# A new replayed order, with smaller edits at the start, in a two-layer kernel of windowed attention and token mixing

## The chip, the cores and the metric

The kernel runs on one core of one Trainium2 chip. The core has five engines that run side by side, each through its own list of instructions: PE (TensorE, matrix products into PSUM), DVE (VectorE), ACT (ScalarE), POOL (GpSimd) and SP (SyncE, which here only issues DMA transfers). They wait for each other by semaphores. The metric is device time in microseconds. Before the change three runs gave 435.66, 436.49 and 438.69 us, median 436.49.

## The reference, cut to what matters

Two layers, each a windowed attention A and a token-mixing block B, on x of 2048 rows by 512, with a residual around each. Types are bfloat16.

```python
def _A_ref(x, wqkv, wo):                      # 32 heads of 16, window 256
    q, k, v = split(x @ wqkv)
    scores = einsum("bhqd,bhkd->bhqk", q, k) * Dh ** -0.5
    scores = where(0 <= i - j < 256, scores, -1e9)
    return einsum("bhqk,bhkd->bhqd", softmax(scores), v) @ wo

def _B_ref(x, w1, b1, w2, b2):                # mixes along the 2048 rows
    u = gelu(einsum("bsd,sf->bdf", layernorm(x), w1) + b1)   # F = 1792
    return transpose(einsum("bdf,fs->bds", u, w2) + b2)

x = x + _A_ref(layernorm(x), wqkv, wo);  x = x + _B_ref(layernorm(x), w1, b1, w2, b2)
# and the same two lines again with the same weights
```

## The kernel before

The 2048 rows lie as 16 tiles of 128 partitions in SBUF (`x_sb`). The attention takes blocks of 512 rows (`prepare(m)`, m = 0 to 3), which `qkv` projects; in layer 0 the first block is done in two halves of 256 rows. For a row tile, DVE makes statistics (`bn_stats` L471, `bn_aggr` L473), POOL the power -1/2 of the variance (`rstd`, L484), DVE the normalised rows (`xh_sb`, L491). The tile is then turned: in the first half by PE (L549) with a copy out of PSUM (L556 on DVE, L558 on ACT), else by a transposing DMA on SP (L542).

Then come the projections: queries (evicted at L572 or L574), keys, values. A key goes into `kbd`, which holds for each of two heads of a partition group a copy with the other head's rows zero, so that one score matmul of 128 columns of weights serves both heads. There are two ways to write it. Directly from PSUM: two operations, one for each half, multiply by the 0/1 column `par` (L583 on DVE, L582 on ACT). Or by way of a staging tile (`evk`, L594 or L596) and then either two such products from SBUF on POOL or DVE (L609), or eight small DMAs (L604) that copy only the rows that aren't zero and rely on the rest having been zeroed: two POOL memsets of a whole key buffer (L461) do that at the start. Values are evicted to `vst` (L631, L633) and spread to `vb` by four DMAs (L636).

The attention of a chunk of four or eight 64-row blocks (`CHUNKS`) is a row of score matmuls (L690), exponentials on ACT (L705), masks by an integer product on POOL or an integer AND on DVE (L726, with the constants `ldm` and `ldn`), and value matmuls (L747), whose result is transposed, scaled and transposed back (L767 to L778), projected by `wo` and added to x. Between score matmuls PE does "fillers": projections, `wo`, and the part of w1's product whose rows are ready (`u_part`). At the end of a layer PE does the rest of w1 and w2 alone.

PSUM has eight banks. A block of scores takes four of them, and they come free when the exponential has read them.

What runs when is no decision of the chip or of a scheduler at build time. Each operation is declared to a graph with its reads and writes and the engines that it may run on (`alts`). The list `ORDER`, packed into text at the top of the file, is then replayed (`replay`): it gives the position and the engine of each of about 2,480 operations. From it follow each engine's list, the buffers of every pool, and the waits. The `cost` and `prio` numbers in the code were for the search that made the list; they do not act here. SP issues transfers in the list's order too, one after the other, each waiting for what it needs.

At the start SP issues the loads of x and of wqkv in pieces. PE runs 36 matmuls of 128 columns on a constant tile (L392) until the first normalised rows are there. DVE builds `par`, `half` (L423, L426) and the mask constants `ldm` (L433, L435 and three times L439) and `ldn` (L454) from the triangle `tri`, which POOL makes.

Of the kernel before, what the change touches and what calls it, by code (L numbers as in the profile page):

```python
# [7 lines left out]
dt = mybir.dt  # L8
ALU = mybir.AluOpType
# [6 lines left out]
    'c-qBQJ&5a87Cw^iym#m24ro9DE$D$>P@zHr1r$&~4;*kn0Tl{p!G#}q!G!|~IH1A-2lN&PwBQ9TIN-tyE*x;-!V50EV3sLdcwrV?xbVUhQ@EI7Sf+5{!o?nq'  # L16
    '$20ciz5Hx8yJyB%_g-CH-SeIAd`ALMAW$=FmRTW@UM>_MC=^Pi;EO_mPE}Ps8;@00Q*G-bFh2xcf8YPD^Jy4{4r?wJVNeNZF(i;5j)u<AALc&kTb8BtuoYXD'
    'EV9&YSZ!4!>!g`bN{ewkFV?-!CZqniE{d#Ft%9xV!b#)(TCEaPYV5=_a)q2Md&JD;Y}-<ZEX(4%qNtz|nGh-nqM(nNFd2`>41lrbFj=oV>y08w5=@sO5l;Q9'
    'E5~t`4k7c4g`?**4MwApcs`k)PYEH@>2%p2_m%ug%J;zU^<}w}Bmj_HTwbUu%%gUDrPRKHF)ZpZ8V-j>IkgT#q9zGxwOWL+*Q6H5QAD5FVugcBIS8UCVtAx5'
    'oJ<&u19$iv7cna1#_*YKJ5^OyJ|z~OtkC_q)3F@aao}aY-|XcJja+V-4ePd#=6Nr5$8=54^GwtKgfnf&d1+c%n=zA#x^CzI129br?M|l+Elo!hRD}YZf_Qqu'  # L20
    'SP)3ERD?p|W-T+p<AlWmmz&J>+$%~ixu#_`=S`xiFBAY-2B_6)1cnJql2x_3URO7ptD9B5K6*wd)Vkd{-aVgQFQ<Q>cFUdVVsW`#OsA3K%;)o&*{hi55Q9-J'
    '&$FfBG&||^{?_aDDLp%bAP7veKNy<kcP63}C9PHz{n0aH$ElgsxDhjE)LBq-b-g0Gt{ca(`sEk$b^TQ&DrE65;-xkz7100?E&w~1%|a*V<m_xVrnDCQ9!bX-'
    'm1YXX*h}M)fU!Om&@okIOl(PvC5<{j12J|S3bq}Tigu~!`;_{gMNNZdeg7q;j;bwzsGwS!B?u~0Ziq%Y!^?{V8oI8Zce{fD0`^>Em^H0dLzbj46plFn<Ww=A'
    'FQK`4LOj>DNP1RH&t|jQXq06s1sG+39kbi*t^uyE!Cc~!i-kgzrhK_Xo{tGG>%nMzHqPfML1rY`Bx!fr#C02P^EJAFZ(cjutY58xXXjs)hPF-A3lBL3pX4lJ'
    'o4RQ@9~cBgQ$#}$1OcwgE@B2$AdHBjArra3DN3SFkg5WD1k-axgz>l%2E(u)1b&%$CBINMT;FsZMb~r1oPiq~IYiJfbj!AeLw#WAgbe9`w0dBuuGqvgRI6$j'
    'Lc4<2z`#YeO+!o3Fn0_>IzT9qQcL7U7do+6@7L?yx^*Vrn%pXe80Su@MFqwhm|>=H;=0V37#a(!ArlQI2rlNJAe`WqOfhG#%;{=H-5W~sx^x5=7q*a+gflh$'
    'eZw$Pt#TZr6a%Qw`y4VQmouyne9JOS0EC7qvVzDPj44PKNl{G8B<pp1eIlAyme0J)%S%H$)eL|an)+N(`aLv4B*F~_HO#v|s2W6@$RDsi$nbjkB_tw<aCUYk'
    '2%!wcfUen!F_|78BN06ngymAB$TM;-Nt5|()|t)vvzaWn&qvv;Tm`7MhvtWaKA@`N30<K-=(ly9A_Jd|R8$)In<f)_y+1(=bS0n$TwlMwx<cq7j=u@(C`omM'
    's+WpyhcVx0`At5b6!LM*{CvrmDw0$xmkNc#rysW*%d#2dEs#FcKqmsA;wpwx&^1K`SfV3>fB;P<6ID1nqf~>FlQsVIBw?qUO$1{_QR7&{n2;j^pNrDz@KvRP'
    'TuK<mIr4oZ1y_!9SyUwYJ76btI<*!T3yU5b?QZw{9Hy=d9K2`0HxPs}^t#>t;Lp8&uVtQFrU}$Q`lqt{ZNl~Yf`ICa&~-Y75XsujO{=A87$B%rB7GV}b(9zY'  # L30
    '!{`(WoNg6MMP0AzkT0PA69N(@pXYm16Wzfq^z*(fYqEw}a{7X?cLkw<Ig%y~Rv3X&ok}t$2N6%!f^;N~$NkaC$qf0x1Uyf>-6bt(Dr%$g90?}?KF5_9Bjq&r'
    '9VRfOm7H#+>+RW`V$C>FkB<j`i7}q|K(_<XYPW`Ah;7)b*Etl+sQ&d=xDeCKb@TZ=swXnG*RcqAC>3m#2FEZ|10}nJyGwXDa!fJMLOcUE@4D;t8rCTF_KdDp'
    '|1^yA<<&pVaphmfWICUu<!>~UB*XY_G#-s?$tqjlN}AScVXSKL*K!D9S_VJ=yjH4~LRu`AgEE#cl(BpvpVe)WwLK4sNQCSM`bXp=iwJ^1G+BAkm!89|;E<#0'
    '5m!-^W`k?os-6+90>f~bsiaDi{tQqkm1!RJ6VNdN6KJ;<Xrpm^*cw#FsDIU@*6DORRU@vZyI^4JQ7JM?MU+}7R=i5t^UGK(hjfISwCi<9P;1@T^KGmPwx6?$'
    '*`}Si72oo#we1*=ty>Z<K|oE*NRs|kQo3VFj-qBWDr2RP%}Py=YhYMbK*X6DDpU<N!bV@P(lwST5xh&(i+Q7GS|c{pKw4GeK!HfSMw)Ln+D&j%-rOMigkF)W'
    'tIbAOU&8!+J`XM&6!y_r8jXS!q*_hOK?T1v(t@EBna)rd<f<%4h$aS4NQ;jOl%l*~OW_w9_o&0&&v3hj+gnZ!duhI<*Czn)Jlx^9hb0`)bV%+FN`XV$Zku+n'
    '%>ZN|?LN&sO}kq=zHOhv-X((zp6<=U-J8*Pa_H5QU5DrIHq7vcHy#^*d!K)d4tMK5e>l${9Ua~EIN<K_y7Py7!t>njX^wjX)W6uc-L~877SOvn4xM=XCjR#3'
    'ffxM4i0An?kYc;%9Wwk|$-{APJ07>ksr#_L-FWzK8n-+D0aDygj{&!b@9tr^=Pk!^+<%y7KZ6b2k1gcj|6*(}X#Cwjf54*cklzn(I)3MF&FvFM_fPP5OiFd)'
    'PDWB$dFT6#-?q>0yM*KRNS1zT!}g1NyGbT<D<hdyr!twhb1?I;1+K~*&h7>o9{)0XkL(?vf4BgDKjPoOZ+@F@{L_OaPq}pBkzPEK;jMa+EjG7q-XVq8Cxq-~'
    'fqY-CA5M)9kj(yDwjO2Pn4mw1SmuWW<UnaM{7ypdNwS?t+e|9Z`@ub6^$)5i|0od;xd4x4`DbU#p|J1k!A{$`U5U8saSyKSuRIv-&+SBsdzd5tlMLqG#I842'  # L40
    'njg9Q>mP6%x*dvl<9p-|jZg3K-1a{$!)bv|s~^WdEIxed;iHG!)%)G|$*<zszX32A5e)'
# [263 lines left out]
def bass_interleave_layers__sliding_block__mixer_token_mlp__prompt_kernel(  # L305
# [29 lines left out]
    with es:  # L335
# [54 lines left out]
        def f_warm(e):  # L390
# [3 lines left out]
        op("vector:wm", lambda e: e.memset(uT[:, 0, 0:P], 1.0), writes=["uT0"], cost=100)  # L394
        op("tensor", f_warm, reads=["uT0"], writes=[warm], cost=2000, prio=-1, cfg="f", cls="f")
# [26 lines left out]
        for h in range(2):  # L422
# [10 lines left out]
        op("vector", lambda e: e.tensor_scalar(ldm[:, 0, :], tri[:, 0:64], half[:, 0:1], 0.0, op0=ALU.mult, op1=ALU.add),  # L433
           reads=["tri"] + HALF, writes=["ld0"])
        op("vector", lambda e: e.scalar_tensor_tensor(ldm[:, 0, :], tri[:, 64:128], half[:, 1:2], ldm[:, 0, :],  # L435
                                                      op0=ALU.mult, op1=ALU.add), reads=["tri", "ld0"] + HALF,
           writes=["ld0"])
        for i, m, c in ((1, 1.0, 0.0), (2, -1.0, 1.0), (3, -1.0, 1.0)):
            op("vector", lambda e, i=i, m=m, c=c: e.tensor_scalar(ldm[:, i, :], ldm[:, 0, :], m, c, op0=ALU.mult, op1=ALU.add),  # L439
               reads=["ld0"], writes=[f"ld{i}"])  # L440
        LD = [f"ld{i}" for i in range(4)]
# [18 lines left out]
        for k in (1, 2):  # L460
            op("gpsimd:zero", lambda e, k=k: e.memset(kbd[:, k].rearrange("p a b c d -> p (a b c d)").bitcast(dt.float32), 0.0),  # L461
               writes=["kz0"], cost=1900)
# [56 lines left out]
        def mm_group(kind, dst, n, mk, reads, cols=512, step=2, prio=None, holds=(), after=()):  # L519

            prio = fprio() if prio is None else prio
            for k0 in range(0, n, step):
                k1 = min(n, k0 + step)

                def f(e, cols32, k0=k0, k1=k1):
                    last = None
                    for k in range(k0, k1):
                        last = matmul(e, cols32, *mk(k), start=(k == 0), stop=(k == n - 1))
                    return last
                rd = reads(k0, k1) if callable(reads) else reads  # L530
                op("tensor:" + kind, f, reads=rd, writes=[dst], cost=mm_cost(k1 - k0, cols), prio=prio, holds=holds, after=after, cfg="f",
                   cls="f", flex=True)


        def qkv(m, before, split, layer):
# [3 lines left out]
            def transpose(i, wide):  # L539
# [7 lines left out]
                def f_tr(e):  # L547
# [4 lines left out]
                op("tensor:ftr", f_tr, reads=[f"xh{t}", "ident"], writes=[ft], cost=4 * 60, prio=fprio(),  # L552
                   holds=[tx], cfg="f", cls="f")
# [6 lines left out]
            def proj(o, which, a, b, wide):  # L560
# [3 lines left out]
                at = lambda: bank(ft)[:, 0:n]  # L564
# [424 lines left out]
```

## Time and profile before

The profiled execution took 436.27 us, of which the profile's span is 434.5 us.

| Engine | busy us | share of the span | instructions |
|---|---|---|---|
| PE | 420.9 | 97% | 6177 |
| DVE | 322.6 | 74% | 629 |
| ACT | 317.0 | 73% | 364 |
| POOL | 187.2 | 43% | 277 |

| Stretch, us | what runs there | PE busy | ACT busy | DVE busy |
|---|---|---|---|---|
| 0 to 10 | loads, first normalisation and projections | 7.29 | 4.71 | 7.08 |
| 10 to 80 | layer 0, attention and projections | 63.60 of 70 | 69.03 | 63.93 |
| 80 to 160 | layer 0, attention and first part of w1 | 79.21 of 80 | 73.07 | 63.53 |
| 160 to 200 | layer 0, the rest of w1, w2 | 40.00 of 40 | 12.10 | 26.31 |

The tables give busy time. A share over the whole span is an average over stretches with different limits, so the stretches come first. Matmuls are pipelined, and their ends are modelled: a busy PE may still wait a little between two matmuls. In the lists that follow, "A <- B" reads "A waited for B". L numbers are lines of the kernel before; of the changed kernel, whose lines moved down, the names are given in words where a line would mislead.

### The profile page before, as it was taken

The numbers are of one execution on the slowest core, as the hardware profiler recorded it, in microseconds if no ns is written. First come the engines' busy times: TensorE is split into PE (matmuls) and PEld (weight loads), VectorE is DVE, ScalarE is ACT, GpSimd is POOL, SyncE is SP. The second block draws the span as 40 slices with busy tenths as digits, with TensorE's granted clock in tenths as the row PEclk, the third lists the DMA queues.
The fourth block names the chain that finished last, engine by engine and source line by source line (L and its number), as shares of the span: only waits on it lengthen the run. The fifth ranks groups of instructions, "written<-read, shape, count | busy, mean of one in ns | idle before, by whom it ended". The sixth has DMA issues, their size and how long they took to land.

```text
span 434.5 us, 14318 instructions
## 1 busy us (share of the span) xinstructions
PE 420.9 (97%) x6177; PEld 188.5 (43%) x6177; DVE 322.6 (74%) x629; ACT 317.0 (73%) x364; POOL 187.2 (43%) x277
## 2 busy tenths in 40 slices
PE   7979989999999999999999999999999999999997
PEld 6534333434444444444444444444434444445443
DVE  7998989779996678556777999989788758422205
ACT  5999999999997953606999999899999870520000
POOL 7788865864664620011465554365435221000000
PEclk9999999999999999999999999999999999999999
DMA  8565262302163257723542282240223262747713
GB/s 237 167 125 88 63 127 37 79 5 49 26 166 83 75 152 211 208 62 88 137 110 52 64 147 64 51 77 11 47 64 99 66 175 69 226 140 213 228 32 115
DMA packets 101850, 46.03 MB, mean 106 GB/s; under 512 B 32156, under 2 KB 101788, under 8 KB 101788
## 3 DMA queue, kind: packets, MB, share of 16 engines
q1 hardware_dynamic: 101788, 45.13, 41.7%
q8 instruction: 49, 0.80, 0.8%
q14 instruction: 13, 0.11, 0.1%
HBM read 33.56 MB, written 2.10 MB: 82 GB/s over the span
## 4 chain that ended last, share of the span: by engine, by line
PE 73%; ACT 18%; DVE 6%; DMA 1%; POOL 1%; issue 0%; SPq 0%
PE PS L513 50%; ACT pt L705 17%; PE PS L868 8%; PE PS L690 8%; PE PS L747 7%; DVE stats L471 1%; DMA vb<-vst 1%; DVE xh_sb L491 1%; DVE pt L726 1%; DVE rl L767 1%; DMA x_sb<-in_A_x_dram 1%; POOL pt L726 0%; DVE stg L594 0%; DVE vst L631 0%; SPq L636 0%
## 5 line engine op out<-in xcount | busy, mean ns | idle before, releaser
L705 ACT ACTIVATE pt<-PS 128x1024 bf16<-128x1024 f32 (+1 forms) x304 | 281.0, 1036 | 13.1 <-PE PS L690 11.9
L726 POOL TENSOR_TENSOR pt<-pt,ldm 128x256 int32<-128x256 int32 (+2 forms) x189 | 125.9, 686 | 101.7 <-ACT pt L705 101.1
L513 PE MATMUL PS<-xhT,wqkv 128*128 128x512 bf16 (+1 forms) x288 | 67.8, 357 | 2.7 <-ACT pt L705 1.9
L513 PE MATMUL PS<-xh_sb,w1b 128*128 128x512 bf16 x280 | 69.9, 381 | 0.1
L513 PE MATMUL PS<-uT,w2b 128*128 128x512 bf16 (+2 forms) x308 | 68.3, 360 | 0.0
L690 PE MATMUL PS<-qT,kbd 32*128 32x64 bf16 (+4 forms) x1552 | 60.2, 247 | 3.1 <-ACT pt L705 2.1
L484 POOL TENSOR_TENSOR rstd<-agg,mhalf 128x2 f32<-128x2 f32 (+1 forms) x33 | 23.8, 722 | 66.8 <-DVE agg L473 66.7
L909 DVE SCALAR_TENSOR_TENSOR x_sb<-PS,bcol,x_sb 128x512 bf16<-128x512 f32 x31 | 22.6, 746 | 38.0 <-PE PS L513 37.7
L690 PEld LDWEIGHTS PS<-qT,kbd 32*128 32x128 bf16 x1552 | 22.7, 92 | 61.7 <-ACT pt L705 45.6
L767 DVE STREAM_TRANSPOSE rl<-PS 128x1024 f32<-128x1024 f32 x32 | 39.9, 1248 | 12.3 <-PE PS L747 12.1
L747 PE MATMUL PS<-pt,vb 64*17 64x128 bf16 (+4 forms) x3104 | 43.6, 248 | 2.4 <-DMA vb<-vst 1.1
L471 DVE BATCH_NORM_STATS2 stats<-x_sb 128x6 f32<-128x512 bf16 x64 | 44.2, 693 | 1.5 <-DMA x_sb<-in_A_x_dram 0.8
L883 ACT ACTIVATE uT<-rl,bcol 128x512 bf16<-128x512 f32 x28 | 18.3, 712 | 33.8 <-DVE rl L879 33.8
L513 PEld LDWEIGHTS PS<-uT,w2b 128*128 128x128 bf16 x308 | 27.5, 98 | 31.1 <-issue 3.2
L747 PEld LDWEIGHTS PS<-pt,vb 64*17 64x17 bf16 x3104 | 31.8, 84 | 17.6 <-issue 7.9
L513 PE MATMUL PS<-uT,pt 128*128 128x512 bf16 x168 | 39.2, 379 | 0.0
L868 PE MATMUL PS<-xh_sb,w1b 128*128 128x512 bf16 x168 | 37.7, 379 | 0.0
L513 PEld LDWEIGHTS PS<-xhT,wqkv 128*128 128x128 bf16 x288 | 24.2, 97 | 30.1 <-issue 6.3
L513 PEld LDWEIGHTS PS<-xh_sb,w1b 128*128 128x128 bf16 x280 | 23.7, 98 | 30.8 <-issue 5.9
L513 PE MATMUL PS<-wqkv,xhT 128*128 128x512 bf16 x128 | 34.2, 381 | 0.2 <-DVE stg L594 0.2
L726 DVE TENSOR_TENSOR pt<-pt,ldn 128x256 int32<-128x256 int32 (+1 forms) x77 | 29.6, 404 | 5.3 <-ACT pt L705 5.0
L513 PE MATMUL PS<-wo_sb,oT 128*128 128x512 bf16 x128 | 32.4, 380 | 0.5 <-ACT pt L705 0.5
(62 smaller groups left out, 340.7 us busy)
## 6 DMA issues: line engine op xcount, KB each, us to landing
w1b<-in_B_w_dram SPq DMA_DIRECT2D x112, 128.0 KB, 2.8
w2b<-in_B_w_dram SPq DMA_DIRECT2D x70, 128.0 KB, 2.8
pt<-in_B_w_dram SPq DMA_DIRECT2D x42, 128.0 KB, 3.0
vb<-vst SPq DMA_DIRECT2D x64, 68.0 KB, 2.1
out_dram<-x_sb SPq DMA_DIRECT2D x15, 128.0 KB, 1.8
x_sb<-in_A_x_dram SPq DMA_DIRECT2D x3, 512.0 KB, 6.2
kbd<-stg SPq DMA_DIRECT2D x80, 16.0 KB, 1.9
wqkv<-in_A_wqkv_dram SPq DMA_DIRECT2D x4, 256.0 KB, 5.4
```

The costliest lines, as they stand in the source:

```text
L471: op("vector:stat", lambda e: e.bn_stats(st[:, 0:6], x_sb[:, t, :]), reads=[f"x{t}"], writes=[("st", i)], cost=dve_cost(512))
L484: op("gpsimd:rstd", lambda e: e.tensor_tensor(rstd[:, t0:t1, 0], agg[:, t0:t1, 1], mhalf[:, 0:1].to_broadcast([P, t1 - t0]), op=ALU.pow), ...
L491: op("vector:xh", lambda e: e.tensor_scalar(xh_sb[:, t, :], x_sb[:, t, :], agg[:, t, 0:1], rstd[:, t, :], op0=ALU.subtract, op1=ALU.mult), ...
L513: return e.matmul(o, lhsT=w, rhs=x, start=start, stop=stop, skip_group_check=True)
L690: last = e.matmul(bank(tt[r // 2], r % 2)[:, base + c0 * 64:base + (c0 + n) * 64], lhsT=kbd[32 * r:32 * r + 32, tk.slot, o, jj].rearrange( ...
L705: op("scalar:exp", lambda e, ts=ts, tp=tp, i=i, cols=cols: e.activation(probs(tp)[:, i, 0:cols, :], pair(ts)[:, :, 0:cols].rearrange("p r ...
L726: return e.tensor_tensor(v, v, m, op=by)
L747: last = e.matmul(bank(t, h)[32 * r:32 * r + 17, i + q0 * 64:i + (q0 + n) * 64], lhsT=vb[64 * h:64 * h + 64, tk.slot, jj, 4 * o + r, :], r ...
L767: op("vector:od", lambda e, t=tod, tr=tr: e.transpose(rl[:, tr.slot:tr.slot + 2].rearrange("p a b -> p (a b)"), pair(t)), reads=[(tod, i) ...
L868: last = e.matmul(bank(tu, tt), lhsT=v()[:, sc - b0, k0 + tt * P:k0 + (tt + 1) * P], rhs=xh_sb[:, sc, :], start=(sc == b0), stop=(sc == NT ...
L883: op("scalar:gelu", lambda e, ft=ft, tt=tt: e.activation(uT[:, ft, :], rl[:, tmps[tt].slot], ACTF.Gelu_apprx_tanh, bias=b1col[:, ft:ft + 1 ...
L909: op("vector:resy", lambda e: e.scalar_tensor_tensor(x_sb[:, t, :], bank(ft), b2col[:, t:t + 1], x_sb[:, t, :], op0=ALU.add, op1=ALU.add), ...
```

## The change

It has five parts.

1. Key buffers are zeroed in part. Instead of two memsets of a whole buffer there are three of half a buffer. The quarter pair (buffer 1, first two head groups) isn't zeroed; its keys in layer 0 may no longer be written by the small DMAs. Each reader now waits for its own half.
2. The mask constants take four operations instead of six, over pairs of the four quarters. The first and the last may run on POOL or on DVE, and the order has them on POOL.
3. The direct eviction of keys on DVE is one product over both halves, with broadcast operands, instead of two operations. On ACT it remains two.
4. Two short groups of matmuls on the constant tile (two and six of 128 columns) are added on PE: between the first two groups of transposes, and ahead of the first key projection. The first half's transposes are declared in reverse.
5. `ORDER` is another list: positions and engines of all operations change, those of the transfers on SP too.

```diff
-            for _ in range(36):
-                last = e.matmul(PS[:, warm.slot, 0:P], lhsT=uT[:, 0, 0:P], rhs=uT[:, 0, 0:P], start=True, stop=True)
+        def f_warm(e, n=36, t=warm):
+            for _ in range(n):
+                last = e.matmul(PS[:, t.slot, 0:P], lhsT=uT[:, 0, 0:P], rhs=uT[:, 0, 0:P], start=True, stop=True)
             return last
+        def warm_more(n, t, key):
+            op("tensor:wm2", lambda e: f_warm(e, n, t), reads=["uT0"], writes=[key], cost=56 * n, prio=fprio(), after=first_tr[-1:],
+               cfg="f", cls="f")
...
-        op("vector", lambda e: e.tensor_scalar(ldm[:, 0, :], tri[:, 0:64], half[:, 0:1], 0.0, op0=ALU.mult, op1=ALU.add),
...
-        for i, m, c in ((1, 1.0, 0.0), (2, -1.0, 1.0), (3, -1.0, 1.0)):
-            op("vector", lambda e, i=i, m=m, c=c: e.tensor_scalar(ldm[:, i, :], ldm[:, 0, :], m, c, op0=ALU.mult, op1=ALU.add),
+        both(lambda e: e.tensor_scalar(ldm[:, 0:2, :], T2(0), half[:, 0:1], 0.0, op0=ALU.mult, op1=ALU.add), "tri", *HALF, w="ld0")
+        op("vector:ldm", lambda e: e.scalar_tensor_tensor(ldm[:, 0:2, :], T2(1), half[:, 1:2], ldm[:, 0:2, :], op0=ALU.mult,
+                                                          op1=ALU.add), reads=["tri", "ld0"] + HALF, writes=["ld0"], cost=240)
+        both(lambda e: e.tensor_scalar(ldm[:, 2:4, :], ldm[:, 0:2, :], -1.0, 1.0, op0=ALU.mult, op1=ALU.add), "ld0", w="ld2")
...
-        for k in (1, 2):
+        for k, o in ((1, 2), (2, 0), (2, 2)):
+            op("gpsimd:zero", lambda e, k=k, o=o: e.memset(kbd[:, k, o:o + 2].rearrange("p a b c d -> p (a b c d)").bitcast(dt.float32), 0.0),
+               writes=[("kz", k, o)], cost=950)
...
+                begin = not layer and t < 2
+                if begin and first_tr:
+                    warm_more(2, ft, ft)
...
+                if wide and which and not layer and not m:
+                    warm_more(6, ft, key)
...
+                    def f_kb(e):
+                        k = [P, n // 64, 2, 64]
+                        return e.tensor_tensor(kbd[:, tk.slot, o, a // 64:b // 64], src().unsqueeze(2).to_broadcast(k),
+                                               par[:].unsqueeze(1).unsqueeze(3).to_broadcast(k), op=ALU.mult)
...
+                if not layer and m == 1 and o < 2:
+                    ways = ways[:-1]
+                zeroed = [("kz", m, o - o % 2)] if not layer and m in (1, 2) and len(ways) == 3 else []
...
-                for i in range(a // P, b // P):
+                for i in range(a // P, b // P)[::-1 if first and not layer else 1]:
```

What the new list does at the start can be read from the built program. On SP the loads come as x1, x0, x 2 to 3, keys and queries (first half of the columns), queries (second half), x 4 to 7, keys (second half), values, x 8 to 11, a piece of w1, the biases, x 12 to 15; before, the second half of keys and queries came after x 4 to 7, and the biases ahead of x 8 to 11. The second group of `vb` transfers stands right behind the four transposing DMAs, ahead of `wo` and a piece of w1; before, it stood behind these. On DVE the middle operation of the mask constants stands ahead of the first normalisation. Of the first two copies out of the transposes one is on DVE, and the first query's eviction too; on ACT the first exponential follows the first key's two operations.

More of the change, by code (lines that the diff above doesn't have):

```diff
@@ L530, in mm_group @@
                 rd = reads(k0, k1) if callable(reads) else reads
[L531 to L532 removed]
+                op("tensor:" + kind, f, reads=rd, writes=[dst], cost=mm_cost(k1 - k0, cols), prio=prio, holds=holds,
+                   after=after, cfg="f", cls="f", flex=True)
         def qkv(m, before, split, layer):
```

84 lines of the change are left out of this document (40 added, 44 removed).

## The prediction

> **What bounds the kernel now.** I read the page's busy shares first, then busy time by stretch, then what TensorE (PE) waits for, then the chain that ended last. The time of one profiled execution is 436.27 us for a span of 434.5 us (1.8 us lie around it); the median of the three runs shown is 436.49 us. I sum against 436.27 and take the two as one. Busy time by stretch (start:end, length, then busy us of each engine, granted TensorE clock, DMA share, GB/s):
>
> ```profile
> 0.00:5.00 5.00, 3.90 (x36) 3.76 (x36) 2.66 (x13) 1.28 (x1) 4.07 (x12) 1.00 0.59 164
> 5.00:10.00 5.00, 3.39 (x43) 2.46 (x42) 4.42 (x15) 3.43 (x8) 3.89 (x7) 1.00 1.01 298
> ...
> 10.00:36.00 26.00, 22.41 (x512) 12.03 (x510) 24.99 (x61) 25.17 (x33) 22.01 (x36) 1.00 0.58 138
> 36.00:80.00 44.00, 41.19 (x835) 16.77 (x832) 38.94 (x74) 43.86 (x49) 31.20 (x44) 1.00 0.45 84
> ...
> 100.00:160.00 60.00, 59.67 (x1207) 26.54 (x1207) 47.79 (x90) 53.47 (x57) 34.25 (x48) 1.00 0.35 91
> 160.00:200.00 40.00, 40.00 (x186) 17.91 (x185) 26.31 (x50) 12.10 (x18) 2.07 (x3) 1.00 0.54 145
> ```
>
> From 100 us on PE has almost no gap; from 10 to 80 us ACT (25.17 of 26, 43.86 of 44) is the bound, with DVE close behind it up to 36 us; before 10 us nothing is full but the DMA engines. So an edit can only win in the first 80 us, where PE stands idle. What it stands idle for, in total, times, longest:
>
> ```profile
> PE PS L513 <- ACT pt L705: 2.4, 6, 0.5
> PE PS L690 <- ACT pt L705: 2.1, 8, 0.6
> PE PS L747 <- DMA vb<-vst: 1.1, 1, 1.1
> ```
>
> The first two say that scores and fillers wait for a PSUM bank that an exponential holds; only the third is a transfer. The DMA queue of SyncE (SP) around it, by the timeline, and then the chain through it (start, length):
>
> ```profile
> 22.98 2.44 SPq L542 DMA_TRANSPOSE xhT<-xh_sb  x1
> 25.47 0.58 SPq L416 DMA_DIRECT2D wo_sb<-in_A_wo_dram  x1
> 26.10 0.50 SPq L803 DMA_DIRECT2D w1b<-in_B_w_dram  x1
> 26.64 2.57 SPq L636 DMA_DIRECT2D vb<-vst  x4
> ```
> ```profile
> 28.60 4.01 DMA vb<-vst
> ...
> 32.65 1.52 PE PS L747 x114
> ```
>
> The second set of value rows lands 4.0 us after its issue, where the median of that line is 2.1, with 512 KB of wo and 128 KB of w1 issued right ahead of it.
>
> **The order, whole.** Both kernels replay a fixed order, so I first compared where work stands. Ahead of a given score matmul I counted the filler matmuls (all but scores and value products) in units of 512 columns. Ahead of the first score: 10 before, 8 after. At 2,304 score columns: 32 and 36. At 4,096: 50 and 50, and from there equal or two to four units apart at every point I looked at up to the end (388 and 392 at the end of layer 0, 1,038 and 1,038 near the end of layer 1), with value products equal. So PE's work past some 35 us stands as it did: the shuffle there moves transfers and the side engines. For the w1 and w2 loads, the least work that PE has between what a load waits for and its reader grows a little in the new order. In the trace of before PE never waits for one of these, so I cost that at **0**; cover is PE's own queue, and a load that came late would cost up to its landing time, 2.8 us in the page.
>
> **The change part by part.**
>
> *Mask constants.* Six operations (L433 to L454) become four. The timeline of before, start, length, engine, line (POOL's line is the second zeroing of keys):
>
> ```profile
> 5.99 1.80 POOL L461 MEMSET kbd<- 128x2048 f32 x1
> ...
> 6.41 1.43 DVE L433 TENSOR_SCALAR ldm<-tri,half 128x64 int32<-128x64 bf16 x1
> ...
> 8.01 0.24 DVE L435 SCALAR_TENSOR_TENSOR ldm<-tri,half,ldm 128x64 int32<-128x64 bf16 x1
> ...
> 8.28 0.40 DVE L439 TENSOR_SCALAR ldm<-ldm 128x64 int32<-128x64 int32 x3
> ```
>
> L433 ends at 7.84, as POOL's memset ends (7.79); its short sisters take 0.13 to 0.24. The chain puts 1.35 us of it before the normalisation of row tiles 2 and 3. Afterwards the first and last product run on POOL; the middle one stays on DVE, now ahead of the first normalisation. POOL's nearest row is L609, 128x256, 0.483 mean; each is half that size, so between 0.24 and 0.48. What is late next: DVE's two statistics, a transposed copy and two aggregates, to about 7.95 (6.48 + 0.40 + 0.65 + 0.4), and POOL's two remaining memsets, about 0.95 each (half of 1.96), from about 5.9 to 7.8. rstd then runs at 8.0 where it ran at 8.18: **-0.2**, not -1.4.
>
> [...]
>
> In the new order the middle product reads tri and ldm and stands on DVE when the last aggregate ends (4.73); POOL's second rstd starts at 4.80 and takes 0.64. If both go, the product costs 0.24 to 0.3 ahead of an xh that had slack of 0.46 behind it, so **0**. If it waits for rstd, it ends at 5.7, and the two xh (0.38 and 0.41) at 6.45 instead of 5.89: **+0.55**. I take 0, as L435 ran 8.01 to 8.25 beside an rstd begun at 8.18, and keep 0.55 for a rival.
>
> *First eviction and first exponential.* One of the two first xhT copies moves to DVE (0.40 at L556 against 0.59 on ACT), and the first query eviction too (0.41). ACT then has before its first exponential one copy, and two key operations, but not the second copy, two q casts and one stg cast. The key operations end near 8.45 as now, the query cast on DVE, behind ldn, near 8.45 instead of 8.9: first exponential at about 8.95 instead of 9.40, **-0.45**. But what was left out comes later into the full stretch of ACT. Up to the 40th exponential ACT has behind its first one: before 2 q casts, 1 key pair, 1 vst cast; after 3 q casts, 1 stg cast, 2 key pairs. By start-to-start in the timeline (q 0.26, stg 0.35, key pair 0.78, vst 0.46) that is 1.76 against 2.69: **+0.93**. Together ACT is 0.5 later where it bounds: **+0.5**.
>
> *Keys evicted by one product.* In layer 0, 256 columns: two TENSOR_SCALAR take 0.83 to 0.88. One TENSOR_TENSOR writes 512 elements from PSUM; nearest rows are L789 (0.67) and L583 at 512 (0.75). In layer 1 1.49 for a pair becomes 1.25 (L767, 1,024 elements from PSUM). So -0.1 to -0.25 each, hidden but in 10 to 36 us, where one stands in the chain: **-0.15**.
>
> *Zeroing.* Three memsets of 0.95 for two of 1.96: POOL does 1 us less. POOL has gaps before it (0.39 before rstd): **0**. The region left out is one whose key writers fill both halves.
>
> *Short matmul groups.* Two and six 128-column matmuls on the warm tile, in PE's gaps of 0.47 and 0.77 before 7.1 us. At 54 ns each (128 columns; 512 take 214 in the full stretch, 40 us for 187) they take 0.11 and 0.32: **0**. The granted clock was 1.00 across these gaps already. At twice that (cold warm-up, 112 ns) they would still fit.
>
> *Transfers.* The second value transfer goes ahead of wo and w1, right behind the transposes. Its wait can go down to nothing (landing at the median 2.1) or stay (issue as late). SP's four transposes end at 25.4, the transfer's own issue is 2.57, so about 28.1 + 2.1 = 30.2 against 31.6 when PE first asked (32.65 - 1.06): **-1.06**. Next late is ACT, which gains its 0.68 gap before the exponential of 34.57. On DVE the second vst cast stands about 0.6 us nearer its transpose (no reciprocal and one cast less between), which serves this. The x rows 8 to 15 are issued up to 4 us earlier; their readers, statistics, are not on the chain.
>
> *DVE as a whole.* To the end of its 12th od transpose it loses 5 masks (three of 0.44, two of 0.27) and about 2 us of constants, and takes on a copy, a cast, a vst cast and a key pair (about 2.2). PE's waits for DVE up to 72 us (rl 0.40, vst 0.35) may shrink: between 0 and -0.75, **-0.35**.
>
> Sum: -0.2 + 0.5 - 0.15 - 1.06 - 0.35 = -1.26, so **435.0 us**, 0.3% less. One per cent (4.4 us) is about what a measurement of this kernel tells from no change: the forecast is inside it.
>
> **The rivals.**
>
> *Nothing is gained (436.3).* The value transfer lands as late behind four transposes, and ACT's 0.5 is eaten by a shorter gap. For: DVE is full to 36 us, and the fourth xh of the next block stands no earlier. Chance 0.12.
>
> *Slower through DVE's constant (437.5).* The product of L443 holds the first xh (+0.55), first exponential at 9.5, ACT carries its +0.93 in full, and the transfer's gain is offset by the later start: 436.27 + 0.1 + 0.93 + 0.2. It decides if POOL's rstd starts first and excludes it. Chance 0.15.
>
> *Slower through shared transfers (438 to 443).* DMA is full from 5 to 15 us (1.01, 1.02). x rows 8 to 11 and a w1 piece, 640 KB, now go out right behind the v weights. If transfers share instead of queueing, v (landed 12.5, first read 12.95) comes 640 KB / 300 GB/s = 2.1 us later, the value path with it: 436.27 + 2.1 - 0.45 = 437.9. With w1 or w2 loads late by 2.8 in the full part, 441 to 443. Against: in the trace, landings follow issue. Chance 0.10, of which 0.07 beyond 1%.
>
> *Much faster (430 to 433).* All of PE's waits from 9.7 to 36 us (3.92) and from 36 to 72 (2.64) go, and not just a fifth: 436.27 - 6.56 = 429.7; two thirds, 431.9. For: a lighter DVE. Against: ACT is full, and its work there grows. Chance 0.13, of it 0.11 beyond 1%.
>
> The forecast (433.5 to 436.0) has the other 0.50.
>
> **How the numbers follow.** Range 431.5 to 440.5: it leaves out the end of the fast rival and the end of the slow one, under 0.2. Faster by over 1% 0.12, slower 0.09 (0.07 and tails of the DVE rival), within 0.79.
>
> **What would show it.** Right: first exponential near 8.95; value wait of PE gone; ACT still full from 10 to 80 us; PE without gaps past 100. Wrong: the product of L443 ends with an rstd; a PE wait for w1b, w2b or wqkv; a granted clock below 1.00 after 5 us; or PE's gaps in 36 to 72 us gone, which the equal order gives no ground for.

## The result: 0.7% slower

| | median, us | all runs | ratio to the kernel before, 95% interval |
|---|---|---|---|
| before | 436.49 | 435.60 to 438.69 (7) | |
| after | 440.13 | 439.19 to 441.16 (7) | 1.0073 [1.0046, 1.0101] |
| after, run once more beside other kernels (before there: 436.78) | 440.36 | 439.61 to 440.78 (6) | 1.0077 [1.0056, 1.0099] |

The forecast was 435.0, faster by 0.3%. The time lies inside the range (431.5 to 440.5), but in its upper end and on the other side of no change. That end of the range was there for shared transfers, which did not happen, so that the time lies in it is luck. The profiled execution took 440.7 us for a span of 439.0; before it was 436.27 for 434.5.

Where the 4.5 us of the span come from is read best from the start of the nth exponential (ACT, the engine that bounds the first 80 us), as a difference to the kernel before. The last two columns are versions that the experiments led to; they are explained there.

| exponential (its start before, us) | after | zeroing behind xh | the same, 18 matmuls fewer ahead |
|---|---|---|---|
| 1st (9.40) | +2.15 | -0.50 | -0.34 |
| 25th (31.87) | +2.66 | 0.00 | +0.16 |
| 35th (41.82) | +2.57 | +0.22 | -0.34 |
| 125th (126.77) | +2.92 | +0.59 | -0.25 |
| 135th (139.06) | +4.38 | +1.45 | -0.18 |
| 175th (224.95) | +4.45 | +1.52 | -0.11 |
| 304th (352.23) | +4.17 | +1.23 | -0.33 |

So the change loses 2.2 us before the first exponential, 0.5 to the 25th, and 1.5 between the 125th and the 135th.

### The profile page after: what moved, and what is told of

It reads as the page before. It is cut to its first block, busy times and chain, and to the rows that moved or that the text cites. A ratio compares the mean times of both kernels' runs of the same rounds, so it can differ in the third digit from the quotient of the medians.

```text
span 439.0 us, 14256 instructions
## 1 busy us (share of the span) xinstructions
PE 414.3 (94%) x6118; PEld 190.2 (43%) x6185; DVE 323.0 (74%) x624; ACT 317.8 (72%) x366; POOL 183.4 (42%) x277
## 4 chain that ended last, share of the span: by engine, by line
PE 73%; ACT 20%; issue 2%; DVE 2%; DMA 1%; POOL 0%
PE PS L518 50%; ACT pt L723 20%; PE PS L886 8%; PE PS L708 8%; PE PS L765 7%; DVE xh_sb L496 1%; DVE rl L785 1%; DMA w2b<-in_B_w_dram 1%; DMA x_sb<-in_A_x_dram 0%; ACT kbd L593 0%; DVE stats L476 0%; DVE qT L583 0%; ACT qT L585 0%; PE PS L392 0%; PE PS L554 0%
## 5 line engine op out<-in xcount | busy, mean ns | idle before, releaser
L744 POOL TENSOR_TENSOR pt<-pt,ldm 128x256 int32<-128x256 int32 (+2 forms) x191 | 126.3, 682 | 107.8 <-ACT pt L723 107.7
L518 PE MATMUL PS<-xh_sb,w1b 128*128 128x512 bf16 x265 | 66.6, 381 | 2.5 <-issue 1.8
L518 PE MATMUL PS<-xhT,wqkv 128*128 128x512 bf16 (+1 forms) x271 | 64.2, 359 | 4.5 <-issue 1.5
L765 PE MATMUL PS<-pt,vb 64*17 64x128 bf16 (+4 forms) x3104 | 43.9, 248 | 2.3 <-issue 0.9
L476 DVE BATCH_NORM_STATS2 stats<-x_sb 128x6 f32<-128x512 bf16 x64 | 42.7, 678 | 0.8
L518 PE MATMUL PS<-uT,pt 128*128 128x512 bf16 x164 | 40.1, 380 | 0.2
L765 PEld LDWEIGHTS PS<-pt,vb 64*17 64x17 bf16 x3104 | 31.8, 85 | 17.4 <-issue 6.5
L886 PE MATMUL PS<-xh_sb,w1b 128*128 128x512 bf16 x165 | 37.4, 380 | 0.2
L744 DVE TENSOR_TENSOR pt<-pt,ldn 128x256 int32<-128x256 int32 (+2 forms) x75 | 28.5, 399 | 8.6 <-ACT pt L723 8.3
L518 PE MATMUL PS<-wqkv,xhT 128*128 128x512 bf16 x118 | 32.3, 381 | 1.2 <-issue 0.6
L518 PE MATMUL PS<-wo_sb,oT 128*128 128x512 bf16 x119 | 31.4, 381 | 1.8 <-ACT pt L723 1.1
```

The source lines that it names most:

```text
L476: op("vector:stat", lambda e: e.bn_stats(st[:, 0:6], x_sb[:, t, :]), reads=[f"x{t}"], writes=[("st", i)], cost=dve_cost(512))
L518: return e.matmul(o, lhsT=w, rhs=x, start=start, stop=stop, skip_group_check=True)
L744: return e.tensor_tensor(v, v, m, op=by)
L765: last = e.matmul(bank(t, h)[32 * r:32 * r + 17, i + q0 * 64:i + (q0 + n) * 64], lhsT=vb[64 * h:64 * h + 64, tk.slot, jj, 4 * o + r, :], r ...
L886: last = e.matmul(bank(tu, tt), lhsT=v()[:, sc - b0, k0 + tt * P:k0 + (tt + 1) * P], rhs=xh_sb[:, sc, :], start=(sc == b0), stop=(sc == NT ...
```

## The profile after

Busy time by stretch, columns as in the table shown of before (busy us of PE, PEld, DVE, ACT, POOL; granted clock, DMA share, GB/s):

```profile
0.00:5.00 5.00, 3.90 (x36) 3.76 (x36) 2.82 (x14) 1.28 (x1) 3.84 (x15) 1.00 0.52 159
5.00:10.00 5.00, 3.33 (x24) 2.42 (x23) 4.45 (x8) 0.75 (x2) 2.81 (x5) 1.00 0.99 306
10.00:36.00 26.00, 21.54 (x488) 13.19 (x492) 24.64 (x61) 24.99 (x36) 19.77 (x32) 1.00 0.52 133
36.00:80.00 44.00, 38.82 (x788) 16.29 (x783) 38.99 (x71) 42.90 (x47) 31.47 (x46) 1.00 0.50 89
...
100.00:160.00 60.00, 56.89 (x1174) 25.50 (x1185) 48.08 (x91) 54.25 (x59) 34.31 (x49) 1.00 0.30 75
160.00:200.00 40.00, 39.69 (x304) 18.37 (x306) 26.53 (x49) 13.45 (x19) 3.37 (x5) 1.00 0.63 175
```

From 5 to 10 us ACT has 0.75 us of work where it had 3.43, PE 24 matmuls where it had 43: the start is late. From 10 to 80 us ACT is nearly as full as before (67.9 us for 69.0). In 100 to 160 us PE has 3.1 us free where it had 0.3. More than half of that is missing records (6118 matmuls for 6177): a version of the kernel before that is as fast (the value transfer alone, below) has 1.7 free there with 6111 records. The rest is a gap shown below. The 1.00 of the clock in the second row misleads: the trace has no clock record before 10.38 us, and the matmuls tell another story (below).

What PE waits for (in total, times, longest):

```profile
PE PS L518 <- issue: 4.8, 30, 0.2
PE PS L518 <- ACT pt L723: 3.0, 8, 0.7
PE PS L554 <- DVE xh_sb L496: 1.7, 2, 1.5
...
PE PS L708 <- issue: 1.3, 1, 1.3
```

The first line is no loss: it is 30 idles of 0.2 or less, and the version just named has the same (5.0, 31). The wait for `vb` (1.06 before) is gone, as forecast, but 0.56 of "issue", a wait for nothing that the profile shows, stands ahead of the same value matmuls. The wait for `xh_sb`, the normalised rows, has grown from at most 0.5 to 1.5 at one place, and 1.3 us of "issue" ahead of a score matmul are new. SP's queue around the value transfer, which now goes right behind the transposes:

```profile
28.61 3.13 SPq L654 DMA_DIRECT2D vb<-vst  x4
31.78 0.60 SPq L422 DMA_DIRECT2D wo_sb<-in_A_wo_dram  x1
```

The first new wait has its cause in these rows of the timeline (start, length, engine, line), the last being PE's:

```profile
4.62 0.31 DVE L443 SCALAR_TENSOR_TENSOR ldm<-tri,half,ldm 128x128 int32<-128x128 bf16 x1
4.79 0.57 POOL L489 TENSOR_TENSOR rstd<-agg,mhalf 128x1 f32<-128x1 f32 x1 [0.23 <-DVE agg L478]
4.85 2.71 DVE L496 TENSOR_SCALAR xh_sb<-x_sb,agg,rstd 128x512 bf16<-128x512 bf16 x2
...
5.58 1.84 POOL L466 MEMSET kbd<- 128x1024 f32 x2
...
7.62 0.61 PE L554 MATMUL PS<-ident,xh_sb 128*128 128x128 bf16 x4 [1.48 <-DVE xh_sb L496]
```

The middle mask constant (L443) took 0.31 beside POOL's `rstd` (0.57): the wait for `rstd` that I had kept for a rival did not happen. But of the two normalisations of `xh_sb` in the third row the first took 0.41 (4.85 to 5.26) and the second 2.17 (5.39 to 7.56). POOL's two zeroing memsets lie over it, and it ends 0.14 behind them. It looks like the hold that the mask constant of the kernel before suffered (L433, 1.43 us against POOL's memset), moved to an operation that PE waits for; the experiments test that.

Behind it PE is slow too:

```profile
8.02 0.85 PE L392 MATMUL PS<-uT 128*128 128x128 bf16 x6
8.79 2.23 PE L518 MATMUL PS<-xhT,wqkv 128*128 128x256 bf16 x12
```

12 matmuls in 2.23 us; before 16 took 1.91. One by one those of 256 columns start 213 ns apart until 10.42 us and 107 ns apart behind it, and the trace's record of the granted clock at 1.00 begins at 10.38 us (before: 5.01).

## The experiments

Theories at the start: the **hold** (the memsets keep DVE's second normalisation waiting, and PE with it), the **clock** (PE's clock comes late, because of the pause or by chance), and the **rest** (the order itself, and PE's gap at 131 us).

### The hold

**Zeroing moved to 46 us.** In the list, two entries stand elsewhere (33 and 34 are the memsets, 283 a product of POOL that waited there for 2.2 us):

```diff
+    for i, j in ((33, 283), (34, 283)):
+        o = out.pop([x[0] for x in out].index(i)); out.insert([x[0] for x in out].index(j), o)
```

> The changed kernel with its last two zero memsets on POOL moved from behind the mask constants to a gap of POOL near 46 us; nothing else differs. Theory of the hold: these two memsets (5.58 to 7.42) hold DVE's second first-half normalisation (2.18 us for 0.41), and PE's pause behind it (1.48) also costs the granted clock until 10.4. Then the normalisation ends near 5.9, the 256-column matmuls of the first projections take 107 to 109 ns, the first exponential starts at 9.0 to 9.5 instead of 11.56, and the time falls by 2 to 2.6 from 440.1 to 437.5 to 438.1, still above 436.5 by what the new order costs later. If the clock is not tied to the pause: matmuls at 213 ns until 10.4, first exponential at 10.2 to 10.7, 438.7 to 439.3. If the start is covered by later work: 440.1, unchanged.

Measured: 439.99 us, ratio 1.0058 [1.0040, 1.0076]. The start was as the theory has it: second normalisation 0.41 us, first exponential at 9.22. Yet the time hardly fell. The memsets started at 43.69. DVE and POOL at the new place, two answers of the timeline:

```profile
43.11 2.57 DVE L496 TENSOR_SCALAR xh_sb<-x_sb,agg,rstd 128x512 bf16<-128x512 bf16 x1
```
```profile
43.69 1.85 POOL L466 MEMSET kbd<- 128x1024 f32 x2
```

The memsets met another normalisation, held it for 2.57 us, and PE waited 1.47 for what DVE does behind it. The miss supports the mechanism: the hold travels with the memsets. (A product of POOL ran beside the first 0.65 us of this normalisation; on what that does, see the end.)

**The kernel before with its second memset earlier**, ahead of the triangle, so that it starts at 5.37:

```diff
+    for i, j in ((36, 22),):
+        o = out.pop([x[0] for x in out].index(i)); out.insert([x[0] for x in out].index(j), o)
```

> The kernel before with its second zero memset moved ahead of the triangle on POOL, so that it starts at about 5.4 beside the second first-half normalisation. Theory of the hold: that normalisation ends with the memset near 7.2 instead of 5.89, the first mask constant is no longer held (0.2 to 0.3 us instead of 1.43), the first exponential starts at 10.7 if the clock stays, 11.5 if the pause of PE costs it, and the time rises by 1.3 to 2.2 to 437.8 to 438.7. If the start is covered by later work, or the hold only shifts from one constant to another: 436.5.

Measured: 439.6 us, 1.0049 [1.0031, 1.0068]; first exponential at 12.32, later than either forecast. DVE's timeline:

```profile
5.46 2.00 DVE L491 TENSOR_SCALAR xh_sb<-x_sb,agg,rstd 128x512 bf16<-128x512 bf16 x1 [0.46 <-POOL rstd L484]
...
7.98 0.23 DVE L433 TENSOR_SCALAR ldm<-tri,half 128x64 int32<-128x64 bf16 x1
```

The hold has moved from the constant (1.43 to 0.23) to the normalisation (0.41 to 2.00), and one entry of the list costs the kernel before 2.1 us by the ratio. In this profile PE's clock also goes for 3.41 us behind the hold (below), which is part of that cost.

**The memsets 0.28 us later.** The order stays; the memsets also wait for the second normalisation:

```diff
-        g.replay(begin_order(len(g.ops)))
+        g.ops[34].deps.append(g.ops[43]); g.replay(begin_order(len(g.ops)))
```

> The changed kernel, its order as it is, in which the two zero memsets on POOL also wait for the second first-half normalisation, so that they start at about 5.9 instead of 5.58. Theory of the hold: that normalisation ends at 5.8 (7.56 in the changed kernel), the first exponential starts at 9.2 to 9.5 (11.56), the exponentials up to the 125th stand within 0.5 of the kernel before, and the time falls by 2.0 to 2.6 to 437.5 to 438.1; what is left above the kernel before is the stall of PE near 131 us (1.25). Rival: the memsets then hold the copy of the second transposed tile (0.42 us, near 6.6) until 7.75, and the first exponential comes at 10.3 to 10.6, time 438.7 to 439.2.

Measured: 437.95 us, 1.0021 [1.0007, 1.0036]. The normalisations on DVE, and POOL's timeline:

```profile
4.85 0.96 DVE L496 TENSOR_SCALAR xh_sb<-x_sb,agg,rstd 128x512 bf16<-128x512 bf16 x2
...
5.34 0.29 POOL L445 TENSOR_SCALAR ldm<-ldm 128x128 int32<-128x128 int32 x1
5.86 1.84 POOL L466 MEMSET kbd<- 128x1024 f32 x2 [0.23 <-DVE xh_sb L496]
7.67 0.73 POOL L489 TENSOR_TENSOR rstd<-agg,mhalf 128x2 f32<-128x2 f32 x1
```

The same memsets, on the same engine, started at 5.86 instead of 5.58. The second normalisation takes 0.41 (both end by 5.81), the first exponential starts at 8.90, and up to the 25th the version stays within 0.5 of the kernel before, level with it at the 25th. Statistics (0.69) and the copy out of PSUM (0.41) run beside the memsets at their usual length, so the rival fell. By the ratios (1.0077 to 1.0021) the hold and what follows from it, a late clock included, cost 2.4 us; the two intervals leave about 1 us to either side.

### The clock

**PE's pause filled**: 16 instead of 2 matmuls between the first two groups of transposes.

```diff
-                    warm_more(2, ft, ft)
+                    warm_more(16, ft, ft)
```

> The changed kernel with 16 instead of 2 matmuls of 128 columns on the constant tile between the first two groups of transposes; memsets as they are. It fills PE's pause (6.1 to 7.6) without filling it over: 16 at 107 ns end at 7.4. Theory that the pause costs the clock: clock 1.00 by about 7 to 8.4, first projections at 107 ns a matmul, first exponential at 10.4 to 10.8 instead of 11.56, time down by 0.8 to 1.2 to 439. Theory that the half clock at the start has nothing to do with this pause: matmuls at 213 ns until about 10.4 as now, 440.1.

Measured: 442.92 us, 1.0114 [1.0086, 1.0143], slower than either theory allowed. In its profile the first rows of x landed 0.5 us later, the normalisation was held as before, the clock came at 10.24, and PE had an "issue" gap of 2.48 us near 38 us, behind which the clock went to 0.50 from 40.96 to 44.38. It settled nothing on the clock; its gap pointed at the next question.

**Short groups of one matmul each**, with the zeroing moved to 46 us:

```diff
-                    warm_more(2, ft, ft)
+                    warm_more(1, ft, ft)
...
-                    warm_more(6, ft, key)
+                    warm_more(1, ft, key)
```

> As the version with late memsets, and the two short matmul groups cut to one matmul each. If the short groups cost and bring nothing: within 0.3 of the version with late memsets, first exponential at the same time within 0.2. If they keep the clock: the clock is lost before the first projections, 213 ns a matmul, about 1 us slower than that version. If they are in the way: 0.3 to 0.5 faster.

Measured: 439.15 us, 1.0042 [1.0025, 1.0059], 0.7 less than with the groups by the ratios, though the intervals overlap. The clock was there at 6.75 (6.63 with the groups): they did not keep it here. Part of the gain is the gap near 131 us (0.54 for 1.26), which again pointed on.

**The changed kernel once more**, for a second profile.

> The changed kernel once more, for a second profile beside these runs. Theory: the second normalisation again 2.1 to 2.2 us, the clock at 1.00 late (7 to 10.5) or, where the grid falls well, by 7; a stall of PE near 131 at the same count; time 0.5 to 0.6% above the version whose memsets wait, 440 to 441.

Measured: 440.36 us; second normalisation held again (PE waits 1.55), 1.00 us of "issue" at 132.2. Its clock records start at 5.98, and busy time cut at the records' own times shows what the chip did:

```profile
2.57:5.98 3.41, 3.11 (x30) 2.84 (x28) 3.01 (x10) 0.00 (x0) 2.77 (x7) 1.00 0.93 260
5.98:9.40 3.42, 1.64 (x20) 1.23 (x18) 3.42 (x7) 0.66 (x2) 1.54 (x2) 1.00 1.01 304
9.40:12.81 3.41, 3.41 (x30) 2.25 (x29) 2.08 (x8) 2.21 (x4) 1.63 (x3) 0.50 1.11 352
12.81:16.00 3.19, 3.18 (x43) 2.30 (x43) 3.19 (x9) 2.91 (x7) 1.47 (x3) 1.00 0.66 210
```

In the records the clock changes only at steps of 3.41 us (in the version with the filled pause it goes again 30.72 us, nine steps, behind its grant; in the first profile of either kernel it stays at 1.00 for 430.08 us, 126 steps). Behind a step in which PE was busy for 1.64 (here), 1.11 (kernel before with the early memset) or 0.97 us (filled pause) it went down to 0.50; it stayed up behind 2.14 to 2.31 (kernel before and two versions of it); it was granted behind 2.76 to 3.41, and not behind 2.40 to 2.69. Where the steps fall differs from run to run: the first grant came at 4.14 to 7.03 in profiles of the kernel before and its versions, at 10.38 and 5.98 in the two of the changed kernel. The changed kernel's late clock at 10.38 is thus in part chance: the step from 3.55 to 6.97, with 2.40 of PE work, held the first part of PE's pause.

**No warm-up**: the later version with 18 warm-up matmuls (below), these of 16 columns instead of 256. The count of instructions is the same, PE stands idle until 5.3.

```diff
-        def f_warm(e, n=18, t=warm, w=2 * P):
+        def f_warm(e, n=18, t=warm, w=16):
```

> As the version with 18 warm-up matmuls of 256 columns, but of 16 columns each: as many PE instructions, while PE stands idle until 5.3. It prices a late clock. Theory: granted clock at 1.00 only from 8 to 11.5 us, first projections at 213 ns a matmul, first exponential 0.6 to 1.4 later than in that version, time 0.6 to 1.4 more. If ACT hides it: the same time within 0.3.

Measured: 437.62 us against 436.12. The clock came at 9.24; the first exponential 0.95 later; the time 1.5 more. From one profile to the other the last exponential is 0.76 later. So a late clock is worth 0.8 to 1.5 us here and isn't hidden. A pause of 1.5 us within one step leaves at most 1.9 of work, where 2.14 kept the clock and 1.64 did not. From that I estimate that the clock is likely to come late or go; in which share of the runs was not measured.

### PE's gaps without a cause

The profile's page counts 49 transfers of the kind "instruction", 16 KB each by the trace's packet records. The trace has some 12,300 matmuls and weight loads of PE, 250 for each transfer, so I take these for PE's instructions. The gaps near 131 us, the one of 2.48 and one of 0.76 at 37.4 each ended 1.3 to 1.6 us behind the landing of such a transfer. (The 0.56 ahead of value matmuls, L765, near 32 to 35 us is in every version of the changed kernel and in none of the kernel before, ends 2.7 us or more behind such a landing, and is not of this kind; its cause was not found.) First I held a full DMA stretch for the reason.

**Five pieces of w1 later**: as the version with the memsets behind xh, and pieces 1007 to 1010 and 1012 stand further back in the list. They were meant to leave the full stretch at 126 to 129.

```diff
+    for i, j in ((1015, 905), (1016, 905), (1007, 905), (1008, 905), (1012, 1082), (1009, 1104), (1010, 1104)):
+        o = out.pop([x[0] for x in out].index(i)); out.insert([x[0] for x in out].index(j), o)
```

> As the version whose memsets wait for the normalisation, and five pieces of w1 (128 KB each) that SP issues at 126 to 129 us go out at 139 to 143 instead, behind two pieces that wait there. Theory that PE's stall near 131 is an instruction transfer held up behind a full DMA stretch (each stall of PE without a cause ended 1.4 us behind the landing of a 16 KB instruction transfer): the stall goes (nothing above 0.3 without a cause from 125 to 140), and the time is 1.0 to 1.4 below the other version, 436.3 to 437. Rivals: the stall belongs to the instructions there, not to the DMA: no difference; or a moved piece lands late for its reader near 147: 0.5 to 2.8 slower.

Measured: 439.37 us, 1.0054 [1.0036, 1.0072]. The edit missed its place. By the list and the trace's transfers in order, the five pieces go out at 155.5 to 157.8 without the move and at 162.3 to 164.6 with it. The nine pieces ahead of the gap go out as they did (122.0 to 126.3, here 121.6 to 125.8), and the DMA share is still 0.99 and 0.91 in 127 to 128, where the instruction transfer starts. So this run says nothing for or against the DMA. Its new wait of 0.9 for w1, at 165, comes from the move. The gap was 1.46 us here and 0.66 without the move, with the same work ahead of it: its length varies from one profile to the next.

What holds in every profile of the changed kernel and its versions with this gap is the place. It falls into the row of 24 score matmuls or the 10 long ones behind it, and the place moves with the number of matmuls that stand ahead:

| version | matmuls ahead, against the changed kernel | instruction transfer, us | PE stops behind | gap, us |
|---|---|---|---|---|
| pause filled | +14 | 132.63 to 133.61 | 9 scores | 0.56 |
| changed kernel, and again | 0 | 130.27 to 131.24; 129.70 to 130.58 | 23 scores | 1.25; 1.00 |
| zeroing at 46 us; behind xh; w1 later | 0 | 129.33 to 130.26; 127.32 to 128.43; 127.65 to 128.53 | 23 scores | 1.26; 0.66; 1.46 |
| groups of one | -6 | 129.92 to 130.88 | 24 scores and 5 long | 0.54 |

23 less 14 is 9, and 23 plus 6 is 29: PE stops at a fixed count of its own instructions. The traces count the same: in each of the seven, 2,337 recorded matmuls lie ahead of the gap. 592 lie ahead of the one of 2.48, ahead of that of 0.76, and ahead of one of 0.44 at 39.8 in the changed kernel. The changed kernel, the first and the fourth row in PE's timeline, one fence each:

```profile
130.97 0.41 PE L708 MATMUL PS<-qT,kbd 32*128 32x64 bf16 x23
132.63 0.21 PE L708 MATMUL PS<-qT,kbd 32*128 32x128 bf16 x1 [1.25 <-issue]
```
```profile
134.13 0.28 PE L708 MATMUL PS<-qT,kbd 32*128 32x64 bf16 x9
134.97 0.35 PE L708 MATMUL PS<-qT,kbd 32*128 32x128 bf16 x15 [0.56 <-issue]
```
```profile
130.51 1.25 PE L518 MATMUL PS<-xh_sb,w1b 128*128 128x512 bf16 x5
132.31 1.25 PE L518 MATMUL PS<-xh_sb,w1b 128*128 128x512 bf16 x5 [0.54 <-issue]
```

My reading is that short matmuls use up what PE has left in 0.4 us, and long ones give the transfer time. That can be tested by the count alone.

**18 matmuls fewer ahead**: as the version with the memsets behind xh; the warm-up is 18 matmuls of 256 columns, as long as 36 of 128.

```diff
-        def f_warm(e, n=36, t=warm):
+        def f_warm(e, n=18, t=warm, w=2 * P):
             for _ in range(n):
-                last = e.matmul(PS[:, t.slot, 0:P], lhsT=uT[:, 0, 0:P], rhs=uT[:, 0, 0:P], start=True, stop=True)
+                last = e.matmul(PS[:, t.slot, 0:w], lhsT=uT[:, 0, 0:P], rhs=uT[:, 0, 0:w], start=True, stop=True)
```

(The short groups keep 128 columns, and the constant tile is set to twice the width.)

> As the version whose memsets wait for the normalisation; the warm-up is 18 matmuls of 256 columns instead of 36 of 128: the same time on PE, 18 matmuls fewer ahead of everything. Theory that PE's stalls without a cause are waits for its own instructions (16 KB transfers that start at the same count of PE instructions in every kernel, about the 4,720th recorded near 127 us and the 1,180th near 35; what PE has left runs out faster where short matmuls follow): all work stands 18 matmuls earlier in the count, 10 long matmuls follow the transfer near 127, and the stall near 130 (0.66 in that version, 1.25 in the changed kernel) goes, time 436.8 to 437.4 where that version has 437.95. If the stall belongs to the scores there: it stays. If the shift only moves the stall to another transfer: one of over 0.4 elsewhere, no gain.

Measured: 436.12 us (435.83 to 436.66, 12 runs), 0.9978 [0.9964, 0.9992]. The same place in PE's timeline:

```profile
127.80 0.41 PE L708 MATMUL PS<-qT,kbd 32*128 32x64 bf16 x24
128.14 2.33 PE L518 MATMUL PS<-xh_sb,w1b 128*128 128x512 bf16 x10
```

No gap, here or near 37 us, where the version without this edit had 0.76 behind an instruction transfer. Matmul by matmul, that version falls 0.92 us behind this one at 37.4 and 0.87 at 129.7, which is the whole difference between the two profiles. This one is 0.43% (1.9 us, each ratio uncertain by 0.6) faster than that, faster than forecast for it, and 0.2% faster than the kernel before.

**The short groups alone, on the kernel before**, two matmuls behind the first four transposes and six behind the second:

```diff
+                    for _ in range((6, 2)[t] if not layer and t < 2 else 0): e.matmul(PS[:, warm.slot, 0:P], lhsT=uT[:, 0, 0:P], rhs=uT[:, 0, 0:P], start=True, stop=True)
```

> The kernel before with the two short groups alone: two matmuls of 128 columns on the constant tile right behind the first four transposes, six behind the second four. Theory that they are free and bring nothing: within 0.3 of the kernel before. Theory that they keep the granted clock where the 3.4 us grid of its records falls badly (kernel before: pauses of 0.47 and 0.77 before 7.1): the slow end of the spread of the kernel before (438 to 439) goes, median 0.3 to 0.8 lower. If they are in the way at half clock (107 ns each): 0.2 to 0.5 slower.

**The same, with 8 matmuls fewer in the warm-up** and as many columns:

```diff
-            for _ in range(36):
+            for w in [P] * 20 + [2 * P] * 8:
```

> The kernel before with the two short groups, and 8 instructions less in the warm-up (20 matmuls of 128 columns and 8 of 256), so that every later instruction of PE stands at its old count. Theory of the instruction transfers: the stalls of the version with the groups alone (0.42 near 130, 0.37 near 162) go, and the time is that of the kernel before, 1.0 to 1.5 below that version. If the groups themselves cost: as that version, 0.34% above the kernel before.

Measured: 438.81 us, 1.0034 [1.0016, 1.0051] with the groups alone, 436.11 us, 0.9984 [0.9967, 1.0001] with the count restored. In the first the 11th to 85th exponentials stand within 0.1 of the kernel before, and then gaps come: 0.42 at 129.8, behind 24 scores and one long matmul, and 0.37 at 162.2; the last exponential is 1.82 late. In the second none of these is left. Compared matmul by matmul, the first falls behind the second at four places from 80 us on: 0.21 at 90.3, 0.36 at 117.0, 0.59 at 129.8 and 0.53 at 162.2. Each lies 1.2 to 1.7 behind the landing of an instruction transfer, and two don't show as an "issue" gap. Eight matmuls that cost nothing where they stand cost 1.5 us (0.34%) 80 to 160 us on, by the count.

### The value transfer

**The kernel before with the second value transfer ahead of wo and w1**, and nothing else:

```diff
+    for i, j in ((15, 431), (837, 431)):
+        o = out.pop([x[0] for x in out].index(i)); out.insert([x[0] for x in out].index(j), o)
```

> The kernel before with the second group of value transfers ahead of wo and of the w1 piece in SP's queue, as the new order has it, and nothing else. The prediction's step: PE's wait for it (1.06) goes and the time falls by 1.06 to about 436.4 where the kernel before is at 437.4. Rival: ACT is the bound there, and the wait hides behind its row of exponentials: 0 to 0.3 gained, exponentials from the 35th on at the same times within 0.3.

Measured: 436.57 us, 1.0001 [0.9981, 1.0021]. PE's wait of 1.06 is gone. Between the 25th and the 35th exponential its profile gains 0.92, by the 304th 0.35 of that is left. The ratio can't tell the result from nothing; it excludes little, as its interval reaches 0.8 us down.

## Why the prediction was wrong

**Zeroing, costed at 0: wrong, and the largest part of the miss.** The step said that POOL does 1 us less and has gaps. It looked at POOL's time and not at whom POOL holds. I had the hold in front of me (L433 ended as POOL's memset ended) and used it only for the constant that was to go; what the memsets would lie over next I took for free ("POOL's two remaining memsets, about 0.95 each", "from about 5.9 to 7.8"). They ran from 5.58 to 7.42, over the second normalisation. Cost with its clock: 2.4 us. 0.28 us decided it: started at 5.86, about where I had put them, they cost no normalisation anything, but I had not asked what an earlier start would do.

The rival "slower through DVE's constant" put the same kind of hold on the wrong pair: product and `rstd` ran side by side (0.31 and 0.57). That a DVE product waits for an `rstd` no run shows. What was held beside POOL's memsets were `tensor_scalar` operations of DVE: L433 (1.43) and the normalisations (2.17, 2.57 and 2.00). The held normalisations of the changed kernel and of the version with zeroing at 46 us started 0.19 and 0.58 us ahead of the first memset, but behind another POOL operation (L445 at 5.34, a product at 43.02). Why DVE is held beside one POOL operation and not beside another, no trace shows.

**Short matmul groups, costed at 0: wrong in a way I had not thought of.** The gaps took them, as the step said. What they cost came from their count: on the kernel before, eight matmuls cost 1.5 us with it and nothing without it. In the changed kernel the gap at 131 is 1.25 us; removing 18 matmuls gave 1.9 us by the ratio, 1.6 from one profile to the other. What its own eight cost there was not measured by itself. My sum had no term for the gaps of 0.4 to 2.5 us behind transfers of the kind "instruction", 16 KB each in the packet records.

**"The granted clock was 1.00 across these gaps already": true for one execution.** Its steps fell well (2.17 of 3.41 us busy over the gaps, and it stayed). I treated one profile's clock as the kernel's.

**"PE's work past some 35 us stands as it did": right, and it missed the count.** The matmuls were equal; the instructions ahead of them weren't.

**Mask constants (-0.2): right in sign.** With the hold out of the way `rstd` of tiles 2 and 3 starts at 7.67 where it started at 8.18.

**First exponential (-0.45, then +0.93 carried): half.** Without the hold it came 0.50 earlier, and what was carried over ate that by the 9th exponential; at the 25th the difference is 0.00, not +0.5.

**Key product: right.** 0.66 for a pair of 0.83 to 0.88, 1.22 for 1.49.

**Value transfer (-1.06): oversized.** The wait went, 0.92 was gained in place on the kernel before and 0.35 kept in the profile, and the time did not change measurably. In the changed kernel 0.56 without a cause stands where the wait was.

**DMA rival: not seen.** PE waits for no w1, w2 or wqkv piece in the profile after.

**DVE as a whole (-0.35): not measured by itself.**

The sum of -1.26 was a forecast for a kernel that has no hold and no stalls by the count. The version with 18 matmuls fewer is closest to it: -0.33 in its profile, -0.22% (1.0 us) by the ratio. Along this path of versions the change is +2.4 for the hold and its clock, +1.9 for 18 matmuls of count, and -1.0 for the rest. The three add up to the 0.77% measured by construction, and each is uncertain by 0.6 to 1.1 us.

## What to carry to other kernels

When an operation is moved or shortened on POOL, list what DVE does in its new place, not only what POOL does, and keep long POOL operations, memsets above all, off the normalisations that PE waits for (2.17 us here for 0.41); a single added wait can do that (0.41 again). Instructions added far ahead of dense short matmuls can cost by their count alone (eight cost 1.5 us here), so filler matmuls are better few and wide (18 of 256 columns for 36 of 128 gave 1.9). The first microseconds should be judged from several profiles, as the clock's steps fall differently in each (at 1.00 from 10.38 and from 5.98 in the two of the changed kernel).

## What the runs showed that I had not expected

- A DVE normalisation is held by POOL operations that were under way when it started, and not by memsets alone. In the profile after, 11 more took 0.49 to 1.05 us; each had begun beside a product of POOL (L744 or L791) and ended 0.15 behind it. (`rstd`, of 128x1, did not hold it: 0.41 from 4.85, beside 4.79 to 5.35.) Between two products in a row it got its turn. Ahead of a memset that followed, and between two memsets, it did not: it started 0.19 us (5.39 and 5.58) and 0.58 us (43.11 and 43.69) before the first and ended 0.14 to 0.15 behind the second.
- Moved 0.28 us, the same memsets cost nothing: statistics of 0.69 and PSUM copies of 0.41 run beside them.
- PE stops at a fixed count of its instructions and goes on 1.2 to 1.7 us after a 16 KB instruction transfer lands. That the count costs time is shown by two pairs of versions (18 fewer, and eight restored on the kernel before); that the late transfer is the reason fits every gap but was not tested by itself. The profile calls it "issue", and twice (0.76 at 37.4, 0.44 at 39.8) put it down to DVE. What sets the start of the transfer was not found, and whether the full DMA stretch delays it was not tested.
- The clock's steps of 3.41 us: it went down behind steps with up to 1.64 us of PE work (48%) and stayed behind those with 2.14 (63%) or more.
- The version with 18 wide matmuls spread over 0.8 us in 12 runs, the kernel before over 3.5 in the 29 beside it. Whether that is the clock was not tested.
